# Splitting a projection's 448 input rows as three times 128 and a shared rest, inside a two-stage kernel

## The chip, the cores and the metric

The kernel runs on one core of one Trainium2 chip. The metric is the device time of one execution in microseconds (us), lower is better; three runs were made of the kernel before. One more execution was recorded by the hardware profiler.

## The reference

Two branches share the input x (1, 2048, 448) and are mixed by a gate.

```
g = sigmoid((x * gate_w).sum(-1))
a = causal convolution of x with K, by FFT of length 4096
    (K from log_A_real, A_imag, C_real, C_imag, log_dt), + x * D_skip
b = _B_ref(x, wq, wk, wv, wo, beta):
    q, k, v = x @ wq, x @ wk, x @ wv        # 16 heads of 28, 4 segments of 512 rows
    per segment: p = softmax(q k^T * scale + mask); a_dot = p v
                 a_mem = phi(q) M / (phi(q) z);  o = sigmoid(beta) a_mem + (1 - sigmoid(beta)) a_dot
                 M += phi(k)^T v;  z += sum phi(k)
    o @ wo
return g * a + (1 - g) * b
```

The three projections x @ wq, x @ wk, x @ wv need more than one rounding to the matmul's input type gives, so x and each weight are split into a high part and a low part (high + low is the number), and a result is the sum of high x high, high x low and low x high.

## The kernel before, in words

The program has two halves. The first (0 to some 420 us) makes the convolution kernel K, and lays three other works into it; the second does attention, the convolution and the output. The change lies in the first.

*The loop of the first half.* `first_half` runs 56 steps. Each computes angles on TensorE (`ps_arg<-ct,lh`, the turns), their sines on ScalarE (`cs<-ps_arg`, `cs<-cs`), products on VectorE (`X`, `Y`), and then sums on TensorE (`ps_k<-Y,X`, 32 rows of the order, printed as x64 in the profile). In this document step n begins with the n-th block of these sums. Four steps make a group. Each group has six exponentials (`EY`, `EX`, from products `ps_arg<-ce,lh`), and since sine and exponential need different tables on ScalarE, a group has a table load before its exponentials and one behind them. The place of the first is called a head here; it lies at the end of steps 6, 10, 14, 18, 22 and so on.

*The projection.* `project` goes through the four segments of 512 rows. It transposes x into `xh` and `xl` (high and low, rows of the transposed x on partitions: four tiles of 112), then makes for each segment eight results of 128 x 512 (`matmuls`, a unit: q or k for four heads, the weights read back from DRAM as tile `w`) and four results of 128 x 450 (`values`, for v and the gate). Each is a sum of twelve products, three for each of the four tiles. A pair of units ends in copies `e` and `hi` on ScalarE, `ph` and `lo` on VectorE. `memory` folds the results into M (`macc`, `tm`).

*The fillers.* `transform_u` is the first stage of the FFT of x: 32 products `ps_m<-ut,s1u`, each with a copy `gs<-ps_m` (ScalarE or VectorE) and a store to `GU`. One such product with its copy is called a filler here.

*What sets the order.* The projection and the fillers are generators. `Feed.spend` is called in each step with a budget in us, and draws pieces of the projection; each piece yields the cost that is booked for it. After the last product of a pair the projection yields "pe" and is held until the next head, where its copies stand directly behind the table load. What is left of the budget then goes to a filler:

```
        if self.due > 1.5 and (self.held or self.done) and self.waiting:
            self.due -= next(self.filling, 0.0)
```

TensorE keeps the order in which the program is written, ScalarE and most of VectorE too in this half (`k.strict`). DMAs are issued by SyncE (SP) from one queue in order. Tiles of the pool take turns in their buffers: `xin` has four (weights at the start, then x, then the copies of four late fillers), `w` two, `gs` three, and the projections' PSUM tile `ps_m` three.

Of the kernel before, what the change touches and what calls it, by code (L numbers as in the profile page):

```python
# [12 lines left out]
F32 = mybir.dt.float32  # L13
F32R = mybir.dt.float32r
# [3 lines left out]
ALU = mybir.AluOpType  # L18
# [5 lines left out]
D = 448  # L24
# [3 lines left out]
SEG = 512  # L28
# [695 lines left out]
def project(nc, k, pp, early, filling):  # L724

    act, copy, v = k.act, k.copy, nc.vector
    gw = pp.tile([112, 4, 2], F32, name="gw")
    nc.gpsimd.memset(gw, 0.0)
    nc.sync.dma_start(gw[:, :, 0], k.gate_w.rearrange("(k p) -> p k", p=112))
    wvh = pp.tile([112, 4, 450], F32R, name="wvh")  # L730
    wvl = pp.tile([112, 4, 450], F32R, name="wvl")
# [6 lines left out]
    nid = early.tile([112, 112], F32R, name="nid")  # L738
    with k.issue_after(k.chained):
        v.tensor_scalar(nid, k.ident[:112, :112], -1.0, None, ALU.mult)  # L740

    def rest(lo, x, hi):

        pt = k.ps("m")[:112, : x.shape[-1]]
        k.mm(pt, k.ident[:112, :112], x, start=True, stop=False)
        k.mm(pt, nid, hi, start=False, stop=True)
        copy(lo, pt, AF.Copy)

    wsp = [pp.tile([112, 4, 2, 4, 32], F32R, name=f"wsp{i}") for i in range(2)]
    for w in wsp:  # L750
        nc.gpsimd.memset(w[:, :, :, :, 28:32].bitcast(F32), 0.0)

    def weights():
        for kt in range(4):
            t = pp.tile([112, D], F32, tag="xin", name="winv", bufs=4)
            nc.sync.dma_start(t, k.wv[112 * kt : 112 * kt + 112])
            for x, n in ((gw[:, kt], slice(448, 450)), (t, slice(0, D))):
                copy(wvh[:, kt, n], x, AF.Copy)
                rest(wvl[:, kt, n], x, wvh[:, kt, n])
            yield 0.3  # L760
        for i, src in enumerate((k.wq, k.wk)):
            for kt in range(4):
                t = pp.tile([112, D], F32, tag="xin", name="win", bufs=4)
                (k.bulk if i else nc.sync.dma_start)(t, src[112 * kt : 112 * kt + 112])
# [92 lines left out]
    def values(s, xh, xl, ts):  # L857
        for t in ts:
            pt = k.ps("m")
            n = 0  # L860
            for kt in range(4):
                for a, b in ((xh, wvh), (xh, wvl), (xl, wvh)):
                    k.mm(
                        pt[:, :450], a[:, kt, 128 * t : 128 * t + 128], b[:, kt],
                        start=(n == 0), stop=(n == 11),
                    )
                    n += 1
# [20 lines left out]
    for s in range(NSEG):  # L888
        if s > 0:
            k.fresh = True  # L890
            yield -next(filling, 0.1)
        xh = pp.tile([112, 4, SEG], F32R, tag="xh", name="xh")
        xl = pp.tile([112, 4, SEG], F32R, tag="xl", name="xl")
        for t in range(4):
            xin = pp.tile([128, D], F32, tag="xin", name="xin", bufs=4)
            with k.issue_after(holds[s]) if s in holds else ExitStack():
                nc.sync.dma_start(xin, k.u[SEG * s + 128 * t : SEG * s + 128 * t + 128])
            pt = k.ps("m")
            for kt in range(4):
                k.tr(  # L900
                    pt[:112, 128 * kt : 128 * kt + 128], xin[:, 112 * kt : 112 * kt + 112], k.ident
                )
            pv = pt[:112].rearrange("p (k q) -> p k q", k=4)
            ts_ = slice(128 * t, 128 * t + 128)
            copy(xh[:, :, ts_], pv, AF.Copy)
            v.tensor_tensor(xl[:, :, ts_], pv, xh[:, :, ts_], ALU.subtract)  # L906
            yield -1.0 if s == 0 or t % 2 else 1.0
        yield from remember()
        if s > 0:
# [556 lines left out]
def gated_mix(ctx, tc, k):  # L1466
# [110 lines left out]
    k.WD = dr.tile([2, 4, 112, 4, 2, 128], F32, name="WD")  # L1577
# [182 lines left out]
```

## Time and profile before

| | |
|---|---|
| median of three runs | 781.15 us (775.3 to 781.82) |
| the profiled execution | 780.51 us, of which the span of the program's instructions is 778.7 |
| PE (TensorE) | 681.5 us busy, 88% of the span |
| DVE (VectorE) | 560.4 us, 72% |
| ACT (ScalarE) | 502.7 us, 65% |
| POOL (GpSimd) | 157.9 us, 20% |
| mean granted TensorE clock | 0.967 |

Times in the profile count from the span's start. A row of a timeline has the start, the busy time, engine, line, operation, out<-in, shape and count, and in brackets the idle time ahead of it with what ended it. A row of the chain (the work that ended last, followed back from the end) has start, duration and what stood there. A row of a window has the busy time of each engine in that stretch with the count of instructions, the granted clock, the share of time in which the DMA engines were busy, and GB/s. Lines such as L1522 and L1476 are helpers through which every matmul or activation goes, so rows are told apart by their tiles.

### The profile page before, as it was taken

To read this page: it belongs to the slowest core of one execution; us is meant where nothing else is said; L and a number is where in the kernel's file an instruction comes from. 1 tells how busy PE (TensorE), PEld (TensorE's weight loads), DVE (VectorE), ACT (ScalarE), POOL (GpSimd) and SP (SyncE) were. 2 spreads that over 40 slices of the span, in tenths; PEclk is the share of its full clock that TensorE was granted. 3 is DMA by queue.
4 is the path that set the end of the run, shared out by engine and by line. 5 is a ranking of instruction groups with operands and counts; after the bars stand their busy time and mean duration, and the time that the engine had idled before them with its cause. 6 is when DMAs were issued, how large, how long until landed. Compare 5 with 4: busy or idle time off the path is not lost.

```text
span 778.7 us, 19775 instructions
## 1 busy us (share of the span) xinstructions
PE 681.5 (88%) x8273; PEld 371.0 (48%) x8289; DVE 560.4 (72%) x758; ACT 502.7 (65%) x621; POOL 157.9 (20%) x193
## 2 busy tenths in 40 slices
PE   1685998999988998889999999898899789979897
PEld 1362555666555665457664444343334334434333
DVE  8989679878899788888875345565555675674486
ACT  4877689889999989988986425665435353451220
POOL 5405300110111101110120002343311221132110
PEclk9998999999999999999999989999999899999899
DMA  9428774234563345733356797999676867556686
GB/s 242 127 71 247 231 250 131 70 106 161 156 219 111 108 126 168 231 130 105 117 211 237 283 323 274 324 333 338 230 233 207 305 208 244 195 195 242 171 266 191
DMA packets 91550, 158.00 MB, mean 203 GB/s; under 512 B 22174, under 2 KB 59542, under 8 KB 91462
## 3 DMA queue, kind: packets, MB, share of 16 engines
q1 hardware_dynamic: 85530, 153.55, 59.9%
q10 hardware_dynamic: 5052, 2.33, 1.2%
q8 instruction: 65, 1.06, 0.6%
q0 software_dynamic: 880, 0.87, 0.4%
q14 instruction: 23, 0.19, 0.1%
HBM read 88.51 MB, written 60.24 MB: 191 GB/s over the span
## 4 chain that ended last, share of the span: by engine, by line
PE 53%; ACT 18%; DVE 14%; DMA 8%; issue 4%; SPq 1%; POOL 1%; ACTq 0%; DVEq 0%; POOLq 0%
PE ps_m L1522 23%; PE ps_c L1522 8%; ACT cs L1476 6%; PE ps_w L1522 5%; PE ps_pv L1522 5%; PE ps_arg L1522 4%; PE ps_mx L1522 4%; PE ps_k L1522 4%; ACT EY L1476 2%; DVE pr L1476 2%; DVE mx L1476 2%; DMA WD<-wsp 1%; DVE xl L906 1%; ACT L1476 1%; DMA V<-VD 1%
## 5 line engine op out<-in xcount | busy, mean ns | idle before, releaser
L1476 DVE TENSOR_REDUCE mx<-ps_mx 128x2 f32<-128x1024 f32 (+3 forms) x128 | 102.4, 821 | 96.2 <-PE ps_mx L1522 93.1
L1476 ACT ACTIVATE PT<-ps_w 128x1024 f32<-128x1024 f32 (+1 forms) x96 | 84.5, 881 | 128.5 <-PE ps_w L1522 119.4
L366 POOL TENSOR_TENSOR EX<-EX,cab 128x1024 f32<-128x1024 f32 x28 | 53.5, 1913 | 288.2 <-ACT EX L1476 266.6
L1476 ACT ACTIVATE cs<-ps_arg 128x1024 f32<-128x1024 f32 x97 | 94.5, 1023 | 3.7 <-DVE Y L414 2.4
L1522 PE MATMUL ps_w<-qu,ku 32*128 32x512 f32 (+3 forms) x768 | 89.5, 350 | 4.6 <-ACT PT L1476 3.3
L1098 POOL TENSOR_SCALAR_AFFINE_SELECT PT<-PT 128x256 f32<-128x256 f32 (+1 forms) x96 | 47.4, 494 | 227.0 <-ACT PT L1476 219.6
L1522 PE MATMUL ps_m<-xh,w 112*128 112x512 f32 x256 | 91.4, 410 | 1.3 <-DMA w<-WD 1.3
L1522 PEld LDWEIGHTS ps_w<-qu,ku 32*128 32x128 f32 x768 | 58.6, 189 | 68.0 <-ACT PT L1476 30.7
L409 DVE TENSOR_TENSOR X<-EX,cs 128x1024 f32<-128x1024 f32 x56 | 69.3, 1238 | 12.6 <-ACT cs L1476 11.8
L1522 PE MATMUL ps_k<-Y,X 128*32 128x64 f32 x3584 | 64.1, 226 | 14.4 <-DVE Y L414 14.4
L1522 PEld LDWEIGHTS ps_k<-Y,X 128*32 128x32 f32 x3584 | 54.9, 113 | 40.4 <-DVE Y L414 22.4
L413 DVE TENSOR_TENSOR Y<-EY,cs 128x1024 f32<-128x1024 f32 x56 | 70.1, 1253 | 0.0
L1476 ACT ACTIVATE cs<-cs 128x1024 f32<-128x1024 f32 x56 | 59.2, 1057 | 1.3
L1522 PEld LDWEIGHTS ps_m<-xh,w 112*128 112x128 f32 x256 | 48.1, 188 | 21.1 <-issue 8.3
L1476 ACT ACTIVATE EY<-ps_arg 128x1024 f32<-128x1024 f32 x52 | 51.3, 1036 | 3.9 <-PE ps_arg L1522 3.7
L1522 PE MATMUL ps_arg<-ct,lh 64*128 64x512 bf16 x224 | 46.4, 384 | 7.0 <-ACT EY L1476 4.9
L1522 PE MATMUL ps_m<-xl,w 112*128 112x512 f32 x128 | 50.3, 393 | 0.0
L1522 PE MATMUL ps_pv<-PT,V 128*32 128x128 f32 (+3 forms) x512 | 46.4, 461 | 4.4 <-DMA V<-VD 4.4
L1522 PEld LDWEIGHTS <-lh 64*128 64x128 bf16 x392 | 20.2, 94 | 59.0 <-issue 46.5
L1522 PE MATMUL ps_m<-wo,pvs 128*128 128x448 f32 x96 | 43.9, 589 | 1.4 <-ACT mn L1476 1.1
L1522 PE MATMUL ps_mx<-ku,qu 32*128 32x512 f32 (+3 forms) x256 | 44.4, 379 | 0.3 <-DMA ku<-KD 0.3
L415 DVE SCALAR_TENSOR_TENSOR Y<-EY,cs 128x512 f32<-128x512 f32 x56 | 40.0, 715 | 3.8 <-ACT cs L1476 2.5
(219 smaller groups left out, 1284.0 us busy)
## 6 DMA issues: line engine op xcount, KB each, us to landing
w<-WD SPq DMA_DIRECT2D x32, 448.0 KB
qu<-QD SPq DMA_DIRECT2D x16, 512.0 KB
ku<-KD SPq DMA_DIRECT2D x16, 512.0 KB
GU<-gs SPq DMA_DIRECT2D x32, 224.0 KB
GK<-gs SPq DMA_DIRECT2D x8, 896.0 KB
gk<-GK SPq DMA_DIRECT2D x16, 448.0 KB
gu<-GU SPq DMA_DIRECT2D x16, 448.0 KB
ks<-ks SPq DMA_DIRECT2D x32, 224.0 KB
```

What stands on the lines that cost most here:

```text
L366: nc.gpsimd.tensor_tensor(o, o, cab, ALU.mult)
L409: v.tensor_tensor(X, ex, t[:, :, 0], ALU.mult)
L413: v.tensor_tensor(Y[:, :, :, :32], lo, y[:, :, :, ::-1], ALU.mult)
L415: v.scalar_tensor_tensor(Y[:, 1, :, 32:], ey[:, :, 32:], -1.0, y[:, 1], ALU.mult, ALU.mult)
L906: v.tensor_tensor(xl[:, :, ts_], pv, xh[:, :, ts_], ALU.subtract)
L1098: nc.gpsimd.affine_select(sl, sl, pat, ALU.is_ge, 0.0, base=0, channel_multiplier=-1)
L1476: x = op(*args, **kw)
L1522: tc.keep_in_program_order(nc.tensor.matmul(*args, **kw))
```

## The change

The 448 rows of x and of the weights are cut as 128, 128, 128 and 64 where there were four times 112. The fourth tile of `xh` holds the high part of the last 64 rows on partitions 64 to 127 and their low part on partitions 0 to 63; `xl` has three tiles. In the weights the last 64 rows stand twice. A result is then three products for each of the first three tiles, one over the whole fourth tile (high and low of x with high weights), and one over its upper 64 partitions (high of x with low weights): eleven. The low part of the last tile comes from one more subtraction on VectorE, the last 64 weight rows from two DMAs. Two of the booked costs are lowered.

```
 def project(nc, k, pp, early, filling):
-    gw = pp.tile([112, 4, 2], F32, name="gw")
+    gw = pp.tile([128, 4, 2], F32, name="gw")
...
+    def rows(queue, t, src, kt):
+        if kt < 3:
+            queue(t, src[128 * kt : 128 * kt + 128])
+        else:
+            for h in range(2):
+                queue(t[64 * h : 64 * h + 64], src[384:])
+
+    def terms(x, w):
+        xh, xl = x
+        wh, wl = w
+        for kt in range(3):
+            yield xh[:, kt], wh[:, kt]
+            yield xh[:, kt], wl[:, kt]
+            yield xl[:, kt], wh[:, kt]
+        yield xh[:, 3], wh[:, 3]
+        yield xh[64:, 3], wl[64:, 3]
...
     def load_w(u):
-        w = pp.tile([112, 4, 2, 128], F32R, tag="w", name="w", bufs=2)
+        w = pp.tile([128, 4, 2, 128], F32R, tag="w", name="w", bufs=2)
...
     def matmuls(u, x):
-        n = 0
-        for kt in range(4):
-            for a, b in ((0, 0), (0, 1), (1, 0)):
-                k.mm(pt, w[:, kt, a], x[b][:, kt], start=(n == 0), stop=(n == 11))
-                n += 1
-            if kt < 3:
+        for n, (a, b) in enumerate(terms(x, (w[:, :, 0], w[:, :, 1]))):
+            k.mm(pt, b, a, start=(n == 0), stop=(n == 10))
+            if n in (2, 5, 8):
                 yield 0.65
...
     def values(s, xh, xl, ts):
-            for kt in range(4):
-                for a, b in ((xh, wvh), (xh, wvl), (xl, wvh)):
...
-                if kt == 1:
+            for n, (a, b) in enumerate(terms((xh, xl), (wvh, wvl))):
...
+                if n == 5:
                     yield 1.2
...
-            yield 1.2
+            yield 1.0
...
-        xh = pp.tile([112, 4, SEG], F32R, tag="xh", name="xh")
-        xl = pp.tile([112, 4, SEG], F32R, tag="xl", name="xl")
+        xh = pp.tile([128, 4, SEG], F32R, tag="xh", name="xh")
+        xl = pp.tile([128, 3, SEG], F32R, tag="xl", name="xl")
...
-            for kt in range(4):
-                k.tr(
-                    pt[:112, 128 * kt : 128 * kt + 128], xin[:, 112 * kt : 112 * kt + 112], k.ident
-                )
+            for kt, c in enumerate((0, 128, 256, 320)):
+                k.tr(pt[:, 128 * kt : 128 * kt + 128], xin[:, c : c + 128], k.ident)
...
             copy(xh[:, :, ts_], pv, AF.Copy)
-            v.tensor_tensor(xl[:, :, ts_], pv, xh[:, :, ts_], ALU.subtract)
+            v.tensor_tensor(xl[:, :, ts_], pv[:, :3], xh[:, :3, ts_], ALU.subtract)
+            v.tensor_tensor(xh[:64, 3, ts_], pv[64:, 3], xh[64:, 3, ts_], ALU.subtract)
...
                 load_w(after[u])
-                yield 0.65
+                yield 0.45
```

The order of the instructions moves with the budget. On TensorE, step 22 (a unit's twelve products between two blocks of sums, ahead of a head) stood before as

```order
L1522 MATMUL ps_k<-Y,X 32x64 x32
L1522 MATMUL ps_m<-xh,w 128x512
L1522 MATMUL ps_m<-xl,w 128x512
L1522 MATMUL ps_m<-xh,w 128x512 x2
L1522 MATMUL ps_m<-xl,w 128x512
L1522 MATMUL ps_m<-xh,w 128x512 x2
L1522 MATMUL ps_m<-xl,w 128x512
L1522 MATMUL ps_m<-xh,w 128x512 x2
L1522 MATMUL ps_m<-xl,w 128x512
L1522 MATMUL ps_m<-xh,w 128x512
L1522 MATMUL ps_k<-Y,X 32x64 x32
```

and on TensorE at the same place it now stands as

```order
L1536 MATMUL ps_k<-Y,X 32x64 x32
L1536 MATMUL ps_m<-xh,w 128x512 x2
L1536 MATMUL ps_m<-xl,w 128x512
L1536 MATMUL ps_m<-xh,w 128x512 x2
L1536 MATMUL ps_m<-xl,w 128x512
L1536 MATMUL ps_m<-xh,w 128x512 x2
L1536 MATMUL ps_m<-xl,w 128x512
L1536 MATMUL ps_m<-xh,w 128x512 x2
L1536 MATMUL ps_m<-ut,s1u 128x448
L1536 MATMUL ps_k<-Y,X 32x64 x32
```

Eleven products are left, and a filler's product has come behind them. The same holds for steps 10, 26, 38 and 42 (there, too, eleven products and a filler); a filler has also come behind the last products of steps 14, 18 and 34.

On ScalarE the head behind that step was, with the sines of two steps (`cs`) ahead of the table load and the copies of the unit pair behind it,

```order
L1476 ACTIVATE gs<-ps_m 128x448
L1476 ACTIVATE cs<-ps_arg 128x2x2x256 x2
L1476 ACTIVATE cs<-cs 128x1024
L1476 ACT_TABLE_LOAD
L1476 ACTIVATE e<-ps_m 128x512
L1476 ACTIVATE hi<-ps_m 128x512
L1476 ACTIVATE e<-ps_m 128x512
L1476 ACTIVATE hi<-ps_m,po 128x512
L1476 ACTIVATE EY<-ps_arg 128x1024 x2
L1476 ACTIVATE EX<-ps_arg 128x1024
```

and ScalarE has at the same head now

```order
L1490 ACTIVATE gs<-ps_m 128x448
L1490 ACTIVATE cs<-ps_arg 128x2x2x256 x2
L1490 ACTIVATE cs<-cs 128x1024
L1490 ACTIVATE gs<-ps_m 128x448
L1490 ACT_TABLE_LOAD
L1490 ACTIVATE e<-ps_m 128x512
L1490 ACTIVATE hi<-ps_m 128x512
L1490 ACTIVATE e<-ps_m 128x512
L1490 ACTIVATE hi<-ps_m,po 128x512
L1490 ACTIVATE EY<-ps_arg 128x1024 x2
```

The filler's copy has come between the last sine and the table load; it is so at all eight heads named. At the end of the first half TensorE had, between the last blocks of sums and the first product of the second half (`ps_w<-kb,s1k`),

```order
L1522 MATMUL ps_k<-Y,X 32x64 x32
L1522 MATMUL ps_m<-ut,s1u 128x448 x3
L1522 MATMUL ps_k<-Y,X 32x64 x32
L1522 MATMUL ps_m<-ut,s1u 128x448 x4
L1522 MATMUL ps_k<-Y,X 32x64 x32
L1522 MATMUL ps_m<-ut,s1u 128x448
L1522 MATMUL ps_w<-kb,s1k 128x448 x4
```

and TensorE now has, from the last piece of the projection (`macc`) to the same product,

```order
L1536 MATMUL ps_arg<-ct,lh_89 128x512
L1536 LDWEIGHTS lh_89
L1536 MATMUL ps_arg<-ct,lh_89 128x512
L1536 MATMUL ps_m<-ph,macc_204 128x512
L1536 MATMUL ps_m<-ph,macc_205 128x512
L1536 MATMUL ps_k<-Y,X 32x64 x96
L1536 MATMUL ps_w<-kb,s1k 128x448 x4
```

The eight fillers of the end are the eight that have come ahead of the heads. From there on the order of all engines is as it was. In SP's queue the load of segment 3's fourth `xin` has moved behind the transposes of the first (it waits for them), since the copies of late fillers, which take `xin` buffers, now lie ahead of these loads.

More of the change, by code (lines that the diff above doesn't have):

```diff
@@ L726, in project @@
     act, copy, v = k.act, k.copy, nc.vector
-    gw = pp.tile([112, 4, 2], F32, name="gw")
+    gw = pp.tile([128, 4, 2], F32, name="gw")
     nc.gpsimd.memset(gw, 0.0)
-    nc.sync.dma_start(gw[:, :, 0], k.gate_w.rearrange("(k p) -> p k", p=112))
-    wvh = pp.tile([112, 4, 450], F32R, name="wvh")
-    wvl = pp.tile([112, 4, 450], F32R, name="wvl")
+    nc.sync.dma_start(gw[:, :3, 0], k.gate_w[:384].rearrange("(k p) -> p k", p=128))
+    for h in range(2):
+        nc.sync.dma_start(gw[64 * h : 64 * h + 64, 3, 0], k.gate_w[384:])
+    wvh = pp.tile([128, 4, 450], F32R, name="wvh")
+    wvl = pp.tile([128, 4, 450], F32R, name="wvl")
     macc = [pp.tile([128, 128], F32, name=f"macc{h}") for h in range(4)]
@@ L736, in project @@
     loaded, holds = {}, {}
-    nid = early.tile([112, 112], F32R, name="nid")
+    nid = early.tile([128, 128], F32R, name="nid")
     with k.issue_after(k.chained):
-        v.tensor_scalar(nid, k.ident[:112, :112], -1.0, None, ALU.mult)
+        v.tensor_scalar(nid, k.ident, -1.0, None, ALU.mult)
+    def rows(queue, t, src, kt):
+        if kt < 3:
+            queue(t, src[128 * kt : 128 * kt + 128])
+        else:
+            for h in range(2):
+                queue(t[64 * h : 64 * h + 64], src[384:])
[8 more added lines that the diff above has]
+        yield xh[64:, 3], wl[64:, 3]
     def rest(lo, x, hi):
-        pt = k.ps("m")[:112, : x.shape[-1]]
-        k.mm(pt, k.ident[:112, :112], x, start=True, stop=False)
+        pt = k.ps("m")[:, : x.shape[-1]]
+        k.mm(pt, k.ident, x, start=True, stop=False)
         k.mm(pt, nid, hi, start=False, stop=True)
         copy(lo, pt, AF.Copy)
-    wsp = [pp.tile([112, 4, 2, 4, 32], F32R, name=f"wsp{i}") for i in range(2)]
+    wsp = [pp.tile([128, 4, 2, 4, 32], F32R, name=f"wsp{i}") for i in range(2)]
     for w in wsp:
@@ L754, in weights @@
         for kt in range(4):
-            t = pp.tile([112, D], F32, tag="xin", name="winv", bufs=4)
-            nc.sync.dma_start(t, k.wv[112 * kt : 112 * kt + 112])
+            t = pp.tile([128, D], F32, tag="xin", name="winv", bufs=4)
+            rows(nc.sync.dma_start, t, k.wv, kt)
             for x, n in ((gw[:, kt], slice(448, 450)), (t, slice(0, D))):
@@ L762, in weights @@
             for kt in range(4):
-                t = pp.tile([112, D], F32, tag="xin", name="win", bufs=4)
-                (k.bulk if i else nc.sync.dma_start)(t, src[112 * kt : 112 * kt + 112])
+                t = pp.tile([128, D], F32, tag="xin", name="win", bufs=4)
+                rows(k.bulk if i else nc.sync.dma_start, t, src, kt)
                 tv = t.rearrange("p (g j e) -> p g j e", j=4, e=28)
@@ L859, in values @@
             pt = k.ps("m")
-            n = 0
-            for kt in range(4):
-                for a, b in ((xh, wvh), (xh, wvl), (xl, wvh)):
-                    k.mm(
-                        pt[:, :450], a[:, kt, 128 * t : 128 * t + 128], b[:, kt],
-                        start=(n == 0), stop=(n == 11),
-                    )
-                    n += 1
-                if kt == 1:
+            for n, (a, b) in enumerate(terms((xh, xl), (wvh, wvl))):
+                k.mm(
+                    pt[:, :450], a[:, 128 * t : 128 * t + 128], b,
+                    start=(n == 0), stop=(n == 10),
+                )
+                if n == 5:
                     yield 1.2
@@ L1576, in gated_mix @@
     k.KD = dr.tile([4, 4, 128, 2, SEG], F32, name="KD")
-    k.WD = dr.tile([2, 4, 112, 4, 2, 128], F32, name="WD")
+    k.WD = dr.tile([2, 4, 128, 4, 2, 128], F32, name="WD")
     k.VD = dr.tile([L, 16, 32], F32, name="VD")
```

3 lines of the change are left out of this document (1 added, 2 removed).

## The prediction

> **What bounds the kernel now.** I read the busy table of the page first: PE leads with 88% of the span, but an average over two halves with different limits says little. So the stretch the change touches was cut into windows, one for each change of pace.
>
> ```profile
> core 0: us, PE busy (x) PEld busy (x) DVE busy (x) ACT busy (x) POOL busy (x), PEclk, DMA share, GB/s
> 137.00:188.00 51.00, 48.01 (x668) 33.69 (x666) 40.48 (x57) 42.49 (x50) 7.65 (x4) 0.97 0.31 101
> 188.00:238.00 50.00, 44.44 (x749) 26.66 (x748) 45.90 (x64) 49.02 (x60) 7.65 (x4) 1.00 0.59 184
> 238.00:287.00 49.00, 46.70 (x663) 31.91 (x663) 41.43 (x60) 43.01 (x50) 7.66 (x4) 1.00 0.34 112
> 287.00:339.00 52.00, 46.09 (x757) 27.26 (x756) 47.05 (x65) 50.74 (x62) 7.65 (x4) 0.99 0.58 184
> 339.00:406.00 67.00, 65.42 (x854) 42.96 (x852) 54.46 (x75) 57.59 (x67) 11.95 (x7) 0.98 0.41 140
> ```
>
> The first half changes hands. In 137 to 188, 238 to 287 and 339 to 406 PE is busy for 94 to 98% and sets the pace; in 188 to 238 and 287 to 339 it is ACT with 98%, and PE idles for 11%. A product removed pays only in the former. Next I followed ACT, then PE, through a head (the place where a group's exponentials begin) of the latter kind.
>
> ```profile
> 207.46 0.53 ACT L1476 ACTIVATE gs<-ps_m 128x448 f32<-128x448 f32 x1
> ...
> 209.85 1.06 ACT L1476 ACTIVATE cs<-cs 128x1024 f32<-128x1024 f32 x1
> 210.94 1.28 ACT L1476 ACT_TABLE_LOAD   x1
> ...
> 214.25 1.96 ACT L1476 ACTIVATE EY<-ps_arg 128x1024 f32<-128x1024 f32 x2
> ...
> 219.93 1.28 ACT L1476 ACT_TABLE_LOAD   x1
> ```
>
> ```profile
> 205.07 0.91 PE L1522 MATMUL ps_m<-ut,s1u 64*128 64x448 f32 x2
> 207.26 1.10 PE L1522 MATMUL ps_k<-Y,X 128*32 128x64 f32 x64 [1.28 <-DVE Y L414]
> ...
> 211.24 1.10 PE L1522 MATMUL ps_k<-Y,X 128*32 128x64 f32 x64
> ...
> 215.35 0.39 PE L1522 MATMUL ps_arg<-ce,lh 64*128 64x512 bf16 x2 [0.20 <-ACT EY L1476]
> ```
>
> ACT has no idle time in these rows. The table load starts the moment the last sine ends, and PE waits for EY behind it: whatever delays that load delays all that follows.
>
> **The change part by part.** *Fewer products.* Products of full height and 512 columns follow each other at (155.04 − 154.57) / 2 = 0.235 us:
>
> ```profile
> 153.68 0.38 PE L1522 MATMUL ps_arg<-ct,lh 64*128 64x512 bf16 x2
> 153.99 0.50 PE L1522 MATMUL ps_m<-xh,w 112*128 112x512 f32 x1
> 154.33 0.40 PE L1522 MATMUL ps_m<-xl,w 112*128 112x512 f32 x1
> 154.57 0.63 PE L1522 MATMUL ps_m<-xh,w 112*128 112x512 f32 x2
> 155.04 0.40 PE L1522 MATMUL ps_m<-xl,w 112*128 112x512 f32 x1
> ...
> 156.66 0.39 PE L1522 MATMUL ps_m<-xh,w 112*128 112x512 f32 x1
> 156.97 1.10 PE L1522 MATMUL ps_k<-Y,X 128*32 128x64 f32 x64
> ```
>
> 32 of 512 columns and 16 of 450 (0.235 × 450 / 512 = 0.206) make 10.8 us. But each result now ends in a product over 64 rows. In the rows above a change of shape costs 0.08 (0.31 from 156.66 to 156.97, and from 153.68 to 153.99), and a return to full height another 0.10 (0.34 from 153.99 to 154.33). No row shows a lone product of 64 rows; the nearest are the pairs beside it, which cost at their ends what any change does. By the new order 26 short products are followed by one of 64 rows (no change more than before), 5 by the sums of ps_k (one more, 0.08) and 17 by full height (0.08 twice and 0.10, 0.27 in all): 5.0 us go back, 5.8 us of PE time are left. The ends are 10.8 (shape free) and 5.8; I take 5.8. [...]
>
> *The fillers.* A filler is one product of transform_u with its copy to gs. The budget is fed with less for each result, and eight fillers that stood behind the last projections now stand earlier. Each takes 0.91 us on PE (205.07), so the first half up to 406 carries 8 × 0.91 = 7.3 more against 5.8 less. Five of them (steps 10, 22, 26, 38, 42) stand after the last products before a head, with the copy on ACT ahead of the table load. The trace has one such place:
>
> ```profile
> 104.14 3.25 PE ps_m L1522 x11
> ...
> 107.41 0.03 ACT gs L1476
> ...
> 107.97 1.28 ACT L1476
> ```
>
> In this chain the load follows the copy's start by 0.56, and the copy the filler's end. At step 22 the products end one earlier, 211.24 − 0.235 = 211.0; the filler's result is there at 211.9, the copy starts at 211.95, the load at 212.5 in place of 210.94: **+1.56**. Behind the load stand e, hi, EY, EX and the load back, all on ACT; nothing hides it. On SP the filler's GU store now stands ahead of the QD and KD stores, for which nothing in this half waits. Steps 10 and 42 repeat this, and 38 lies as they do:
>
> ```profile
> 127.99 1.10 PE L1522 MATMUL ps_k<-Y,X 128*32 128x64 f32 x64 [0.81 <-DVE Y L414]
> 131.66 1.28 ACT L1476 ACT_TABLE_LOAD   x1
> 329.82 1.10 PE L1522 MATMUL ps_k<-Y,X 128*32 128x64 f32 x64 [1.28 <-DVE Y L414]
> 333.50 1.28 ACT L1476 ACT_TABLE_LOAD   x1
> ```
>
> From sums to load is 3.67 and 3.68 there, 3.68 at step 22. Step 26, where DVE also runs full, is put at the same. Five heads: **+7.8**. The bounds are 0.45, a copy alone, and 1.56.
>
> The filler at step 14 ends at 161.8 by the same steps, and its load moves from 158.71 to 162.3:
>
> ```profile
> 158.71 1.28 ACT L1476 ACT_TABLE_LOAD   x1
> ...
> 170.15 0.39 PE L1522 MATMUL ps_arg<-ct,lh 64*128 64x512 bf16 x2 [0.90 <-ACT EY L1476]
> ```
>
> This stretch belongs to PE, so the delay shows only in the EY waits: the turns at 170.15 come at about 172.3 (+2.1), with four V products more behind them, so the next step is 1.15 shorter. The copy ahead of the following head adds 0.45: **+1.4**. The fillers at steps 18 and 34 end before ACT is free and cost a copy, 0.45 (18 is counted in the 1.4).
>
> *PE's own stretches.* By the new order steps 4 to 6 hold five products fewer, −1.2, and shapes give back 0.35 (one return to full height, one change ahead of ps_k): −0.8. The V products of the start: 4 × (0.27 − 0.206) = +0.3. Segment 2 (238 to 287) holds three V and two others fewer, 1.1, and has four returns to full height, 1.1; the copy at the head behind it lies partly under PE: 0, with 0.45 as upper end. Segment 3 (339 to 406) holds three V and eight others fewer, 2.5; shapes take 1.3, and some 0.2 is lost where ACT leads: −1.0. Together **−1.5**.
>
> *The split of the input.* xl shrinks to 384 elements, and a subtraction of 64x128 joins it, on DVE, in the chain at each segment's start.
>
> ```profile
> 143.40 1.20 DVE xl L906 x2
> ...
> 227.05 0.21 DVE tm L854
> ```
>
> A full one takes 0.60 and 128 elements 0.21, so 384 take about 0.47 by the line through both: 0.68 against 0.60, four times a segment, 0.3; four segments **+1.2**. The xh copies are as wide as before.
>
> *Loads.* w grows from 448 to 512 KB.
>
> ```profile
> PE ps_m L1522 <- DMA w<-WD: 1.3, 1, 1.3
> ```
>
> PE waits for a w once in this half, for 1.3 us, and an eighth more of that is 0.2 at most; the other loads start a unit ahead: 0. In segment 3 the fourth xin is now issued only when the first is transposed, since fillers hold its buffers:
>
> ```profile
> 65.55 6.35 DMA WD<-wsp
> ...
> 125.94 2.26 DMA GU<-gs
> ```
>
> GU is as large as an xin. With 0.4 for the issue it lands 2.7 after the first transposes, where PE wants it after 2.1; some of that lies under EY: **+0.3** (bounds 0 and, by WD's 6.35, 4.7).
>
> *The tail.* Here the chain ran through the last fillers.
>
> ```profile
> 416.78 0.55 DVE gs L1476
> ...
> 418.39 1.03 PE ps_k L1522 x64
> ...
> 420.40 0.55 ACT gs L1476
> ```
>
> ```profile
> 430.86 0.50 PE L1522 MATMUL ps_mx<-ku,qu 32*128 32x512 f32 x2 [0.31 <-DMA ku<-KD]
> ```
>
> Without them the last sums follow DVE at 416.8: −1.6, and ps_w stands 1.6 earlier; the loads of ku and qu no longer queue behind eight GU stores on SP, which takes away PE's 0.3 wait for ku too: **−1.9** (bounds −1.6 and −3.5).
>
> The sum: 7.8 + 1.4 − 1.5 + 1.2 + 0.3 − 1.9 = **+7.3**. The profiled execution took 780.51 (778.7 of span), so 787.8; the median of 781.15 lies 0.6 higher. I say **788**. The second half stands in the same order and is taken as unchanged.
>
> **Rivals.** *The copies hide* and cost 0.45 at each head: 5.6 less, and 1 less at step 14: 781. For it: DVE waits at 207.26 show that the steps ahead have room on PE. Against: those waits stand before the products, and the filler behind them.
>
> *PE paces the whole half* (88 to 98% busy in every window): the fillers fill its idle time, the products count in full: 780.5 − 5.8 − 1.9 + 1.2 = 774, with free shapes 769. Against it speaks ACT's 98% in two windows.
>
> *Slower: the fourth xin.* If the load takes over 2.1 us to land, PE stands at its transposes, and the exponents and turns behind them wait too. At WD's 6.35 this adds 4.7 − 0.3 to the sum: 792. DMA's share of 0.41 in that window, lower than the 0.59 and 0.58 ahead of other heads, speaks for a quick landing.
>
> **How the numbers follow.** The forecast gets 0.5 (its own range 783 to 792, for the half-hidden heads and the tail's bounds), the hidden copies 0.2, PE as pace 0.17, the late load 0.13. From 776 to 793 holds about eight in ten. Over 1%, about what a measurement of this kernel can tell, means above 789 or below 773.3: 0.5 × 0.45 + 0.13 = 0.36 slower; PE as pace mostly lands near 774 and below, 0.15 faster; 0.49 within.
>
> **What would show it.** At steps 10, 22, 26, 38 and 42 a copy to gs stands before the table load on ACT, waits for PE and moves the load by 1.5; the ACT windows grow by about 3 us each, the PE windows hardly change, and PE's idle time before the last sums is gone. If ACT shows no wait at those copies, the first term falls; if the windows of PE shrink by 3 or more, the shape prices do.

## The result and the profile after

The changed kernel takes **839.74 us** (median of 4 runs, 837.57 to 846.19), the kernel before 781.09: a ratio of 1.078, interval 1.070 to 1.086. The forecast was 788, with a range to 793, so it missed by 52 us. Executions of some kernels below come in two groups about 30 us apart, told apart by the granted clock; the ratios compare the lower group where there is one.

The row of the page that answers best is the one for the clock that was granted to TensorE, in 40 slices of the span. First the kernel before, then the changed one:

```profile
PEclk9998999999999999999999989999999899999899
```

```profile
PEclk9988999999998999989995555999999979998899
```

Four slices in the middle stand at 5: the clock is halved there. The windows of the changed kernel, cut near the starts of the same steps as those of the prediction (12, 19, 28, 35, 44 and 53), and then from the half clock on:

```profile
144.00:196.00 52.00, 48.56 (x656) 31.35 (x648) 40.05 (x59) 40.88 (x48) 7.66 (x4) 0.99 0.30 102
196.00:252.00 56.00, 46.48 (x757) 27.22 (x756) 49.72 (x67) 52.36 (x65) 7.65 (x4) 0.99 0.59 194
252.00:304.00 52.00, 49.30 (x649) 31.97 (x648) 39.47 (x59) 41.11 (x47) 7.66 (x4) 0.95 0.31 105
304.00:360.00 56.00, 46.57 (x787) 27.40 (x788) 49.44 (x68) 52.65 (x66) 7.65 (x4) 1.00 0.51 170
360.00:431.00 71.00, 67.09 (x834) 40.86 (x826) 55.20 (x79) 57.89 (x68) 11.94 (x7) 0.95 0.43 147
438.50:524.00 85.50, 81.00 (x455) 34.30 (x447) 20.17 (x30) 18.46 (x22) 3.03 (x4) 0.50 0.49 178
```

The windows are cut at whole us. By the starts of the steps, the stretches in which ACT sets the pace grew by 5.2 and 3.1 us (steps 19 to 28 and 35 to 44), and those of PE by 1.7, 3.9 and 4.5 (12 to 19, 28 to 35 and 44 to 53). That makes the first half longer; the start of step 53 moves from 406.15 to 430.89, **+24.7**: 2.9 at the start, 8.9 at the five heads, 9.1 where three segments start (steps 12, 28 and 44: 1.6, 3.9 and 3.7), and 3.8 elsewhere. Short stretches of half clock are in these numbers: between the first sums and step 53 they add up to 23.0 us in the changed kernel and to 10.7 before. The last window is the other part: the clock is 0.50 in it for 85 us, while PE is busy for 81.00 of 85.50. From the first product of kb on, the second half of the changed kernel and that of the kernel before, each in one window:

```profile
444.70:835.50 390.80, 353.83 (x3237) 151.25 (x3249) 205.25 (x270) 145.52 (x192) 74.50 (x129) 0.86 0.69 231
```

```profile
420.60:778.70 358.10, 322.89 (x3237) 141.05 (x3249) 204.43 (x276) 147.50 (x196) 74.99 (x129) 0.95 0.75 253
```

The same 3237 records of products keep PE busy for 31 us more, at 0.86 of the clock in place of 0.95, and the window is 32.7 us longer. PE's timeline shows where it begins (start, busy time, what, and in brackets the idle time ahead):

```profile
434.59 1.10 PE L1536 MATMUL ps_k<-Y,X 128*32 128x64 f32 x64
438.08 1.60 PE L1536 MATMUL ps_k<-Y,X 128*32 128x64 f32 x64 [2.40 <-DVE Y L414]
441.56 1.93 PE L1536 MATMUL ps_k<-Y,X 128*32 128x64 f32 x64 [1.88 <-DVE Y L414]
444.75 3.36 PE L1536 MATMUL ps_w<-kb,s1k 32*128 32x448 f32 x8 [1.26 <-DVE kb L436]
```

```profile
413.36 1.10 PE L1522 MATMUL ps_k<-Y,X 128*32 128x64 f32 x64 [0.71 <-DVE Y L414]
...
416.04 1.02 PE L1522 MATMUL ps_m<-ut,s1u 64*128 64x448 f32 x2 [0.36 <-ACT gs L1476]
417.37 1.02 PE L1522 MATMUL ps_m<-ut,s1u 64*128 64x448 f32 x2 [0.31 <-DVE gs L1476]
...
420.68 1.77 PE L1522 MATMUL ps_w<-kb,s1k 32*128 32x448 f32 x8 [0.31 <-DVE kb L436]
```

The second fence is the same place before, where fillers stood and no wait was longer than 0.71. With them gone, PE waits 2.40, 1.88 and 1.26 us. The trace's record of the clock falls to 0.5 at 438.5, behind the first of these waits, and the first products of kb (x8, four products of the program with two records each) take 3.36 us in place of 1.77. It returns to 1 only after 85.33 us. That is 25 times 3.413 us, the shortest stretch of half clock inside this trace and that of before (141.55 to 144.96 here, 136.63 to 140.04 before); the shares of 3.41 us below are taken over this length.

The forecast heads look as they were drawn. ACT at step 22 of the changed kernel:

```profile
218.58 1.06 ACT L1490 ACTIVATE cs<-cs 128x1024 f32<-128x1024 f32 x1
221.01 0.54 ACT L1490 ACTIVATE gs<-ps_m 128x448 f32<-128x448 f32 x1 [1.37 <-PE ps_m L1536]
221.58 1.28 ACT L1490 ACT_TABLE_LOAD   x1
```

The copy to gs stands between the last sine and the table load and waits 1.37 us for PE; before, the load followed the sine at once.

### The profile page after: what moved, and what is told of

Read it like the earlier page. It is cut to its first block, busy times and chain, and to the rows that moved or that the text cites. A ratio compares the mean times of both kernels' runs of the same rounds, so it can differ in the third digit from the quotient of the medians.

```text
span 835.5 us, 19728 instructions
## 1 busy us (share of the span) xinstructions
PE 716.9 (86%) x8225; PEld 375.2 (45%) x8241; DVE 566.5 (68%) x773; ACT 502.4 (60%) x622; POOL 156.5 (19%) x193
## 4 chain that ended last, share of the span: by engine, by line
PE 57%; ACT 14%; DVE 13%; DMA 7%; issue 4%; SPq 1%; ACTq 0%; DVEq 0%
PE ps_m L1536 22%; PE ps_c L1536 9%; PE ps_w L1536 7%; PE ps_pv L1536 5%; PE ps_mx L1536 4%; PE ps_k L1536 4%; PE ps_arg L1536 4%; ACT cs L1490 2%; ACT L1490 2%; DVE Y L413 2%; DVE pr L1490 2%; ACT EY L1490 1%; DVE pvs L1490 1%; ACT hi L1490 1%; DVE mx L1490 1%
## 5 line engine op out<-in xcount | busy, mean ns | idle before, releaser
L1536 PE MATMUL ps_m<-xh,w 128*128 128x512 f32 (+1 forms) x256 | 91.9, 429 | 2.8 <-DMA w<-WD 2.7
L1536 PE MATMUL ps_k<-Y,X 128*32 128x64 f32 x3584 | 66.5, 230 | 16.3 <-DVE Y L414 16.1
L1536 PEld LDWEIGHTS ps_k<-Y,X 128*32 128x32 f32 x3584 | 56.9, 116 | 43.1 <-DVE Y L414 24.9
L1536 PEld LDWEIGHTS ps_m<-xh,w 128*128 128x128 f32 (+1 forms) x256 | 44.6, 187 | 32.1 <-issue 21.0
L1536 PE MATMUL ps_arg<-ce,lh 64*128 64x512 bf16 x168 | 35.0, 396 | 20.9 <-ACT EY L1490 15.6
L1536 PEld LDWEIGHTS <-lh 64*128 64x128 bf16 x392 | 22.1, 94 | 63.9 <-issue 50.1
L1536 PE MATMUL ps_mx<-ku,qu 32*128 32x512 f32 (+3 forms) x256 | 47.6, 404 | 0.0
```

Of the source, the lines that this page charges most:

```text
L1536: tc.keep_in_program_order(nc.tensor.matmul(*args, **kw))
```

## The experiments

**Theory 1**: fillers that no longer stand among the last sums let PE idle, the clock halves, and the second half starts at half speed. **Rival**: the new tiles make the second half late for another reason, and the clock only follows. The change has two parts that can be set apart, the tiles (three of 128 rows and a shared one) and the booked times, which place the fillers.

### The new tiles with the old booked times

```
-                yield 0.45        (a unit)
+                yield 0.65
-            yield 1.0             (a V result)
+            yield 1.2
```

> The changed kernel with the two booked times put back (0.65 a unit and 1.2 a V result), so that the fillers stand where they stood before: eight of them among the last sums, none added ahead of a table load. The three tiles of 128 rows and the eleven products stay. Theory 1 (clock: without fillers PE idles 2.4, 1.9 and 1.3 us between the last sums, the granted clock halves and stays at 0.5 for 85 us): the long half clock goes, the stretch from the last sums on is again about 344 us long (it was 348 before, 401 after, both from step 53 on), 32 us less, and the heads give back 8.9: about 799. What is left above 781 is then the tiling's. Rival (the second half starts late for another reason that the new tiles bring, such as loads or the place of buffers, and the clock only follows): the heads' 8.9 come back and nothing else, about 831.

Measured: 796.35 us, ratio 1.018 (1.013 to 1.024). Its clock row has no half stretch in the middle:

```profile
PEclk9989999999999999989999989999999799989699
```

So 43 of the 59 us go with two booked numbers; the rival falls. Three of the four executions lie at 794.88 to 796.43; the fourth took 827.43, with a granted clock of 0.919 against 0.954 to 0.959, so the half clock has become rare here and not impossible. Step 53 begins at 413.46, 7.3 later than before: this is what the tiles cost the first half, in spite of 48 products fewer. From step 53 on this kernel takes 380.6, 8.1 more than before, with 51 us of short half-clock stretches against 38; the run after next, with the same tiles, takes 370.4 there, so these 8.1 us are no fixed price of the tiles, and what brings them stays open. Its heads cost nothing (steps 10 to 12, 22 to 24, 26 to 28, 38 to 40 and 42 to 44 together −0.5 us against before).

### The old tiles with the new booked times

```
-                yield 0.65
+                yield 0.45
-            yield 1.2
+            yield 1.0
```

> The kernel before, with the two lower booked times alone (0.45 a unit, 1.0 a V result): old tiles of 112 rows, twelve products, but the fillers drawn earlier and none left for the last sums. Theory 1 (clock): the half clock at the start of the second half appears here too, +32, and the heads add some 8 to 9: about 821. Rival (the new tiles make the second half late): only the heads, about 789.

Measured: 834.25 us, ratio 1.067 (1.061 to 1.072), 13 more than theory 1 had asked for and 45 more than its rival. Its last sums and its clock:

```profile
430.18 1.10 PE L1522 MATMUL ps_k<-Y,X 128*32 128x64 f32 x64 [2.41 <-DVE Y L414]
433.65 1.93 PE L1522 MATMUL ps_k<-Y,X 128*32 128x64 f32 x64 [2.38 <-DVE Y L414]
```

```profile
PEclk9588999999999999999985555999999889998699
```

The same waits and the same half clock, from 431.9 on and again for 85.33 us, with none of the new tiles. The first half is 16.8 longer than before, of which the five heads make 9.7. From step 53 on it takes 408.9, 36.3 more than before. With the run before, the parts add up in the first half: 7.3 + 16.8 = 24.1, where both together gave 24.7.

### Products that nobody reads among the last sums

```
             feed.fill(2)
+            k.turn_over(k.ps("m"), 8)
...
     feed.fill(4, False)
+    k.turn_over(k.ps("m"), 6)
     sums(2 * NJ - 1)
+    k.turn_over(k.ps("m"), 4)
```

> The changed kernel, and 8, 6 and 4 products of 128x512 bf16 whose result nobody reads, on PE ahead of the last two sums and behind them, where PE waits 2.40, 1.88 and 1.26 us. Fillers stay where the change put them. Theory 1 (clock): the long half clock goes, about 32 us less, 808; the first half keeps its +24.7. Rival (late for another reason): 840, or a little more.

Measured: 803.21 us (799.09 to 809.52), 36.5 less than the changed kernel. PE there:

```profile
431.29 1.90 PE L1539 MATMUL ps_m<-ct,one 128*128 128x512 bf16 x8
433.46 1.10 PE L1539 MATMUL ps_k<-Y,X 128*32 128x64 f32 x64 [0.28 <-DVE Y L414]
434.50 1.47 PE L1539 MATMUL ps_m<-ct,one 128*128 128x512 bf16 x6
437.21 1.10 PE L1539 MATMUL ps_k<-Y,X 128*32 128x64 f32 x64 [1.25 <-DVE Y L414]
...
439.48 1.77 PE L1539 MATMUL ps_w<-kb,s1k 32*128 32x448 f32 x8 [0.20 <-DVE kb L436]
```

Added work makes the kernel faster. The products of kb are back at 1.77 us. From step 53 on this kernel takes 797.0 − 426.6 = 370.4 us, before 372.6, the changed kernel 404.6. This shows theory 1: what was missing there was work on PE, not anything that the fillers compute.

### Only the first of the three waits filled

The first added line of the diff above alone.

> The changed kernel with 8 products that nobody reads in the first of the three waits alone (2.40 us, ahead of the sums before the last); the waits of 1.88 and 1.26 us behind it stay. If the first wait alone makes the clock fall: the long half clock goes, about 808. If any of the three is enough, or the two that are left together: it stays, about 840, and begins one or two windows later than 438.5.

Measured: 834.96 us. The record has the half clock from 441.0 on, for 78.51 us, behind the wait that is left:

```profile
436.40 1.10 PE L1537 MATMUL ps_k<-Y,X 128*32 128x64 f32 x64 [0.74 <-DVE Y L414]
439.88 1.10 PE L1537 MATMUL ps_k<-Y,X 128*32 128x64 f32 x64 [2.37 <-DVE Y L414]
442.21 3.35 PE L1537 MATMUL ps_w<-kb,s1k 32*128 32x448 f32 x8 [1.23 <-DVE kb L436]
```

The record falls just as the wait of 1.23 begins, so in this trace the fall needed no long wait ahead of it but the one of 2.37 us.

### A dense run of products at the start of the second half

```
+    turn_over(16)
     first = transform_k(nc, k, tp)
```

> The changed kernel, nothing added at its last sums, so PE waits there as before and the clock halves; but 16 products of 128x512 bf16 that nobody reads stand at the start of the second half, ahead of the first product of kb. Theory A (the half clock lasts because the work behind it, products over 32 rows with one such full product for every eight, is too light to bring the clock back): the clock returns to 1 one to three windows of 3.41 us later, the stretch at 0.5 is 7 to 14 us long in place of 85.33, and the time is 839.7 + 16 x 0.43 = 6.9 - 32 = about 815. Theory B (the stretch of 85 us is a fixed time once it has begun, whatever PE does in it; it was 85.33 in two kernels and 81.92 in a third): 840 + 7 = 847.

Measured: 807.93 us, ratio 1.030 (1.022 to 1.038).

```profile
441.67 1.93 PE L1537 MATMUL ps_k<-Y,X 128*32 128x64 f32 x64 [2.08 <-DVE Y L414]
443.93 4.27 PE L1537 MATMUL ps_pv<-wz 128*128 128x512 bf16 x15 [0.33 <-issue]
448.13 1.77 PE L1537 MATMUL ps_w<-kb,s1k 32*128 32x448 f32 x8
```

The clock falls at 438.9 as ever (sums of 1.93), and is back after 6.83 us: the products of kb take 1.77. So the 85 us are no fixed time. This points to the work itself as what kept the clock low: products over 32 rows, with one full product (128x512) after every four of them (x8 in the profile). The last experiment tests it. Where the stretch is left alone, its end belongs to a place in the program: in all nine traces that have it (75.09 to 92.16 us long) it ends 8.6 to 13.2 us after the first product `ps_w<-qu,ku` of attention, where full products stand closer together (three to five in its last 3.41 us).

### The eleventh product over all rows

```
-        yield xh[64:, 3], wl[64:, 3]
+        yield xh[:, 3], wl[:, 3]
```

> The changed kernel with the eleventh product over all 128 rows of the fourth tile in place of its last 64 (the lower 64 rows add low times low, which the kernel otherwise leaves out). No product of 64 rows is left in a result, so the shape changes that the prediction priced at 5.0 us of PE time go. If that price was right, of which under half lies where PE sets the pace: 2 us less, about 838. If shapes cost nothing: 840. If the shape changes are what makes the first half longer by 24.7 beyond the heads: 824 to 830. The half clock of the second half stays by either theory.

Measured: 837.52 us (824.92 to 840.05), where the changed kernel has 839.74 (837.57 to 846.19); the ranges overlap, and the half clock stays (from 439.3, for 81.92). This run alone settles nothing on shapes: the stretch from its first sums to step 5 is 3.1 us longer than in the changed kernel, with short dips of the clock in it.

### One subtraction in place of two

```
-            v.tensor_tensor(xl[:, :, ts_], pv[:, :3], xh[:, :3, ts_], ALU.subtract)
-            v.tensor_tensor(xh[:64, 3, ts_], pv[64:, 3], xh[64:, 3, ts_], ALU.subtract)
+            v.tensor_tensor(xl[:, :, ts_], pv, xh[:, :, ts_], ALU.subtract)
...  (behind the four tiles)
+        nc.gpsimd.tensor_copy(xh[:64, 3], xl[64:, 3])
```

with the booked times of before, xl with four tiles, and the eleventh product over all rows.

> The changed kernel with the booked times of before (as the first run), the eleventh product over all 128 rows, and the split of the subtraction undone: one subtraction of 128x512 into an xl of four tiles on VectorE, and one copy of 64x512 a segment on GpSimd that puts the low parts beside the high ones in the fourth tile. Nothing of the result is left out. If what the tiling costs is the split on VectorE, each pair 0.89 us against 0.60, four pairs a segment with ScalarE and PE waiting behind them and the clock halved by that wait at the last segment's start (1.3 and 1.9 us there), then the first half gives back 1.2 at each segment start and up to 2 more at the last one, and the shapes 2: some 5 to 7 less than the 796.35 of the first run, about 790. If the tiling's cost lies elsewhere (the start's loads, 2 us; the clock in the second half, 8 us): 795.

Measured: executions of 777.23, 780.48 and 780.63, and seven of 807 to 814. Against before, the lower group has a ratio of 0.997 (0.991 to 1.003): no difference, where 790 was expected. The traced execution is of the upper group, so its first half can be read (step 53 at 401.89, **−4.3** against before), and at its end the half clock, which came in spite of the fillers:

```profile
409.98 1.45 PE L1536 MATMUL ps_m<-ut,s1u 64*128 64x448 f32 x4 [0.16 <-ACT gs L1490]
411.63 1.02 PE L1536 MATMUL ps_m<-ut,s1u 64*128 64x448 f32 x2 [0.20 <-ACT gs L1490]
413.07 1.18 PE L1536 MATMUL ps_m<-ut,s1u 64*128 64x448 f32 x2 [0.43 <-DVE gs L1490]
414.18 1.93 PE L1536 MATMUL ps_k<-Y,X 128*32 128x64 f32 x64
```

The clock falls at 413.8, though no idle time is longer than 0.43 and PE is busy for 82% of the 3.41 us before, all of it with fillers, products over 64 rows. The kernel before has a stretch of the same 82% in its trace (413.1 to 416.5, by the same count), with a block of sums beside the fillers, and keeps its clock. It too fell into the upper group now and then, in 4 of the 36 runs made beside this kernel and the next three. What decides between the two at the end of the first half these traces do not show.

### The same with a short eleventh product

The kernel above with `yield xh[64:, 3], wl[64:, 3]`, as in the change.

> The kernel of one subtraction, but with the eleventh product over 64 rows as in the change; fillers and booked times of before. It separates the two parts of the 11.6 us by which the first half up to step 53 was shorter with one subtraction and full height (-4.3 against before) than with neither (+7.3). By the prediction's shape prices (0.17 to 0.27 a result, 5.0 in all, not all of it where PE sets the pace) the first half comes out at -4.3 + 2 to 4, between -2 and 0; if the split subtraction is all of it, at -4.3; if the shapes are most of it, at +3 or more.

Measured: 790.87 us; five executions lie at 788 to 793 (ratio 1.012, interval 1.007 to 1.016) and two, the traced one among them, at 821 to 823. Step 53 begins at 408.59. The starts differ by short dips of the clock (the first sums at 72.60 here, 70.16 in the first experiment, 69.75 with full height), so the distance from the first sums to step 53 is compared, each from one traced execution with the dips in it: before 338.24, two subtractions and short product 343.30, one subtraction and short product 335.99, one subtraction and full height 332.14. **The split costs 7.3 us, the shapes 3.9**, both from single traces. How far such a distance moves by itself can be read from kernels with the same first half: 331.1 to 332.1 in the kernel of one subtraction and full height and the three below that build on it, 338.2 and 340.3 in the kernel before and its control below, and 357.4 to 360.1 in the changed kernel and the three that only add products at the end of the first half or behind it. So the 7.3 is clear, and the 3.9 is good to some 2 us. Why the split costs so much, from DVE (first experiment, then before) and ACT (first experiment) at the last segment's start:

```profile
347.23 0.56 DVE L919 TENSOR_TENSOR xl<-ps_m,xh 128x384 fp32r<-128x384 f32 x1 [0.33 <-ACT xh L1490]
347.80 0.29 DVE L920 TENSOR_TENSOR xh<-ps_m,xh 64x128 fp32r<-64x128 f32 x1
348.12 0.56 DVE L919 TENSOR_TENSOR xl<-ps_m,xh 128x384 fp32r<-128x384 f32 x1
```

```profile
342.61 1.29 DVE L906 TENSOR_TENSOR xl<-ps_m,xh 112x512 fp32r<-112x512 f32 x2 [0.21 <-ACT xh L1476]
343.81 1.28 DVE L1476 CAST xh<-ps_m 112x512 fp32r<-112x512 f32 x2
```

```profile
353.39 1.02 ACT L1490 ACTIVATE cs<-ps_arg 128x1024 f32<-128x1024 f32 x1 [1.66 <-DVE cs L386]
```

A pair takes 348.12 − 347.23 = 0.89 in place of (343.81 − 342.61) / 2 = 0.60. Four pairs delay the step behind them on DVE by 1.3 (it starts 4.90 after the first subtraction, before 3.60), ACT waits 1.66 for it, PE behind ACT, and behind these waits the clock halves for V's products, too:

```profile
357.73 0.58 PE L1536 MATMUL ps_m<-wvl,xh 128*128 128x450 f32 x1
358.10 0.58 PE L1536 MATMUL ps_m<-wvh,xl 128*128 128x450 f32 x1
...
360.11 0.38 PE L1536 MATMUL ps_m<-wvh,xl 128*128 128x450 f32 x1
360.33 0.36 PE L1536 MATMUL ps_m<-wvh,xh 128*128 128x450 f32 x1
360.62 0.47 PE L1536 MATMUL ps_m<-wvl,xh 64*128 64x450 f32 x1
361.02 0.73 PE L1536 MATMUL ps_m<-xh,w 128*128 128x512 f32 x2
```

They follow each other at 0.37 here and at 0.22 further down. Step 44 alone is 3.2 us longer than before. The last rows are also the shape price, measured: 0.29 into a product of 64 rows, 0.40 out of it to full height.

### Keeping the clock between the last sums

Products that nobody reads between the fillers, in the kernel of one subtraction and, as the control, in the kernel before:

```
             feed.fill(2)
+            k.turn_over(k.ps("m"), 4)
...
     feed.fill(4, False)
+    k.turn_over(k.ps("m"), 4)
     sums(2 * NJ - 1)
```

> The kernel of one subtraction and full height (booked times and fillers of before), with 4 products of 128x512 bf16 that nobody reads ahead of each of the last two sums, between the fillers there. Its first half was 4.3 us shorter than that of the kernel before up to step 53, but most of its executions held the half clock for 82 us behind fillers over 64 rows in a window that PE filled to 82%. If rows count as well as busy time for the clock, the products over 128 rows keep it up: all executions about 781 - 4.3 + 1.2 for the added products on PE, 778, the profiled one included, and none near 812. If the long half clock there is chance and not brought by what PE does in these windows, most executions stay at 808 to 814.

> The kernel before with the same 4 and 4 products ahead of its last two sums, as the control: old tiles, twelve products. PE loses up to 1.2 us to them. If the gain of the kernel beside it is the tiling's, this one stands at 781 to 783; if it comes from a better clock behind the last sums alone, this one gains the same, 777 to 778.

Neither did what was expected. The first has 5 of 12 executions at 809 to 814 (the others 778.75 to 788.9, ratio 1.003, interval 0.999 to 1.007). The control has 7 of 12 at 806 to 814, more often than the kernel before itself. The added products go into a ps_m tile and wait for a copy to gs to free it, so they bring an idle time of 1.59 us of their own. But the control's trace shows that the clock did not fall there:

```profile
416.27 1.02 PE L1524 MATMUL ps_m<-ct,one 128*128 128x512 bf16 x3 [1.59 <-ACT gs L1478]
424.50 1.77 PE L1524 MATMUL ps_w<-kb,s1k 32*128 32x448 f32 x8 [0.63 <-ACT gs L1478]
426.74 3.36 PE L1524 MATMUL ps_c<-kb,s1k 32*128 32x448 f32 x8 [0.47 <-issue]
```

The record stands at 1 until 426.2, ten us later, although PE was busy for only 63% of the 3.41 us from 412.55 on, which hold most of that wait. It falls behind 3.41 us (from 422.79 on) that PE filled to 81%: the end of the sums, one filler, a wait of 0.63 and the first products of kb over 32 rows. In the trace of the first of the two kernels the wait of 1.59 brings a short dip of 3.41 us, and the long stretch begins at the same place as in the control. What brings the fall there, and whether rows count in it, these two runs do not settle.

### Dense or spread

The last two kernels are that of one subtraction and full height with 16 products more at the start of the second half, once all in one row and once spread over it:

```
+    turn_over(16)
     first = transform_k(nc, k, tp)
```

```
     (in the 16 steps of transform_k)
-        turn_over(1)
+        turn_over(2)
```

> The kernel of one subtraction and full height, and 16 products of 128x512 bf16 that nobody reads at the start of the second half, ahead of the first product of kb. They cost 16 x 0.215 = 3.5 us of PE at the full clock. If light work at the start of the second half is what keeps a half clock once it has come (in the changed kernel the same 16 products ended it after 6.83 us), no execution holds it for 75 us or more, and all lie at 778.5 + 3.5, 780 to 786. If the half clock can also begin behind them, in the products over 32 rows themselves, part of the executions stay at 810 to 816.

> The kernel of one subtraction and full height, and in the 16 steps of transform_k at the start of the second half two full products that nobody reads in place of one. 16 more of them, at 0.215 us 3.5 in all, as in the kernel beside it, but spread between the products over 32 rows. If the share of full products in this stretch decides whether the clock stays or comes back, the long half clock goes here too and the executions lie at 780 to 786. If only a dense run of full products brings the clock back, part of them stay at 810 to 816.

Measured: the dense run 782.88 us, all 12 executions within 778.54 to 789.86; the spread ones 816.48 us, 7 of 12 at 816 to 820 and the others at 780 to 787. The traces, dense first:

```profile
417.64 1.86 PE L1537 MATMUL ps_m<-ut,s1u 64*128 64x448 f32 x2
419.43 5.72 PE L1537 MATMUL ps_pv<-wz 128*128 128x512 bf16 x16
```

```profile
417.79 3.35 PE L1536 MATMUL ps_w<-kb,s1k 32*128 32x448 f32 x8
421.08 1.03 PE L1536 MATMUL ps_pv<-wz 128*128 128x512 bf16 x2
```

Both had fallen to half clock before (1.86 for one filler, of 1.02 at the full clock, and 3.35 for the first products of kb). The run of 16 ended it 6.83 us after it began; two full products after every four small ones (x8) left it for 92.16 us. So here a dense run of full products brought the clock back, and the same number spread out did not.

No version beats the kernel before. With the dense run all 12 executions lie below 790, but its 16 products cost some 3.5 us of PE at the full clock (an estimate, 16 × 0.215 by the rows of 8 and of 6 above: 1.90 − 1.47 for two) against the 2.3 to 4.4 that the first half wins in the four traces that share it (4.3 in the one above): 782.88 against 782.61 for the kernel before on the same chip, ratio 1.004 (1.000 to 1.008).

## Why the prediction was wrong

**The step that failed** is the tail, and with it the sentence that the second half "is taken as unchanged". The missing fillers were priced as a pure gain of 1.9 us, and the only reason given for the rest was that the second half's order stays. Counted from step 53 to the first product of kb, the gain is 0.7 (14.53 before, 13.86 after); the price is 32.7 us behind it. The prediction followed waits and chains and looked at the granted clock only where it stood at 0.97 to 1.00; none of its rivals had it fall. The hint was in the profile of before: fillers filled PE's time between the last sums, and what follows there is products over 32 rows. "PE's idle time before the last sums is gone" was even named as a sign that the forecast was right; the idle time became larger (2.40, 1.88 and 1.26 against 0.71, 0.36 and 0.31 at most).

The first half was too low as well, and by itself it would have left the stated range. The terms up to step 53 are 7.8 + 1.4 − 1.5 + 1.2 + 0.3 = +9.2, and +24.7 was measured. Of the 15.5 us between them the split has 6.1 and the start 2.6; the other terms follow below. Some 5 us belong to no term. The prediction had none for the clock in this half either, and 12 us more of half clock are in it; how much of the 5 is theirs was not tried.

Of the fall itself the traces show this much: the longest idle time at this place of the changed kernel was 2.40 us, and the clock then stayed at 0.50 for 85.33 us, while PE was busy for 81.00 of the 85.50 in the window around them. The lengths of 6.83, 78.51, 81.92 and 85.33 us are 2, 23, 24 and 25 times 3.413, the length of the shortest stretch.

**The heads**: right. Five heads were put at +7.8; between the steps that bound them the changed kernel shows 2.0, 1.7, 2.6, 1.7 and 0.9 = 8.9, the old tiles with the new booked times 9.7, the new tiles with the old ones −0.5. At step 22 the load follows the sums by 221.58 − 216.16 = 5.42, before 3.68: +1.74 against the 1.56 forecast. Step 14 was put at +1.4; from step 13 to 21 it is 0.9. The rival in which the copies hide falls.

**The split of the input**: the mechanism was right, the size wrong. +1.2 in all was forecast from a line through two lengths (0.68 a pair); a pair takes 0.89, and the chain behind it costs more than its own time: 7.3 by the difference of two runs. This, more than the shapes, is where the eleven products lost.

**The shapes**: right in price. 0.08 into a short product and 0.18 more out of it were forecast. The rows show 0.29 − 0.206 = 0.08 and 0.40 − 0.206 = 0.19. The whole was put at 5.0 us of PE time; taking it away gave 3.9 of the first half, to some 2 us.

**PE's own stretches**: −1.5 was forecast. The new tiles with the old booked times show −0.4 from step 45 to 53 and −0.25 from 4 to 6, and +0.2 from 29 to 35, −0.5 in all. The rival in which PE paces the whole half falls: 10.8 us of products taken away gave 6.1 from the first sums to step 53 even without split and shapes.

**The start** was forecast with +0.3 and came 2.9 later at the first sums. It was between −1.0 and +4.7 in the other traces, with short dips of the clock at various places; what the wider loads have in it was not tried. The **late fourth xin** is small: the step at that segment's start is 3.7 us longer in the changed kernel and 3.2 in that with the old booked times, which leaves 0.5 for it; in the old tiles with the new booked times, where the split is not, the step is 1.0 longer.

## What to carry to other kernels

Before work is taken away from the stretch ahead of a phase of small products, look at what TensorE does there and at the clock row: here the clock stayed at 1 where fillers stood in the trace of before (341.4 to 460.9), and without them waits of 2.40, 1.88 and 1.26 us came with a second half 32.7 us longer. Work over few rows followed, and a dense run of 16 full products ahead of it, written to a PSUM tile that nobody holds, brought the clock back after 6.83 us; 16 more of the same products spread out did not, in 7 of 12 executions. Here the run cost about what it saved. And an operation split in two can cost more than its parts at its place in the chain: here a pair took 0.89 us where one subtraction took 0.60, and the first half 7.3 more. Price it from a row of the small size, not from a line through larger ones.

## What the runs showed of the hardware

- The clock stayed at 0.50 for 75.09 to 92.16 us in nine traces, with PE busy for 95 to 99% of the time, on products over 32 rows with few full ones between them; 16 full products in a row ended it after 6.83 us in both traces that have them at the start of the second half.
- Neither the busy share of the 3.41 us before nor the longest idle time in them told alone whether it fell. In the traced kernel of one subtraction and full height it fell behind 82%, all over 64 rows, with no idle time over 0.43 us; in the same trace it stayed at 1 behind 70% with an idle time of 1.03, products over 128 rows and the turns (396.73 to 400.15). In the control it stayed at 1 behind 63% and fell behind 81%, as told above. How much the rows count beside the idle time stays open.
- A subtraction of 64x128 from PSUM took 0.29 us on DVE and one of 128x384 0.56, where one of 112x512 went every 0.60.
